# Running the gate and val products of a fused attention and SwiGLU kernel in the quarters of the TensorE array

## The chip, the core and the metric

The kernel runs on one core of one Trainium2 chip. Times are device microseconds of one launch; where a kernel was run several times, the median is given. The profile is one further execution, taken by the hardware profiler; its span reaches from the first to the last instruction and is a little shorter than the time of the launch.

## What is computed

Sigmoid attention over 8 batches, 12 heads, 448 positions and head size 64, and then a SwiGLU block over the 3584 rows that come out of it:

```python
scores = scale * np.matmul(q, k.transpose(0, 1, 3, 2)) - np.log(S)   # S = 448
attn = 1.0 / (1.0 + np.exp(-scores))
x = np.matmul(attn, v)                     # -> 3584 x 768, heads side by side
g = x @ w_gate                             # 768 x 1536
silu = g * (1.0 / (1.0 + np.exp(-g)))
out = (silu * (x @ w_val)) @ w_out         # w_out 1536 x 768
```

Inputs and output are fp32; the products run in 16-bit types and accumulate in fp32.

## The kernel before

The work is cut into small operations (a group of matmuls, one activation, one transfer). Each is noted with its engine, an assumed duration, what it depends on and which buffers it takes and gives back. A list scheduler in the kernel then orders them for each engine at build time, and they are issued in that order[...].

TensorE is used in two ways. Scores and the product of attention with v contract or emit only 64, so four matmuls of 64x64 run side by side in the quarters of the array:

```python
def burst(ds):                     # scores of one or two blocks of 64 keys, 4 heads
    for i, s in ds:
        sc = psum.tile([128, 2, 512], FP32, tag="A", bufs=2, name="ps_sc")
        for g in range(2):
            for a in range(2):
                r = slice(64 * a, 64 * a + 64)
                nc.tensor.matmul(
                    out=sc[64 * (g ^ a):64 * (g ^ a) + 64, a, 0:S]...,
                    lhsT=kT[r, s, 64 * g:64 * g + 64], rhs=qT[r, :, 64 * g:64 * g + 64],
                    start=True, stop=True)
# sig: one ScalarE sigmoid per score tile, PSUM -> pt (fp16)
# pv:  28 quarter matmuls, lhsT = v16, rhs = pt, into two banks of tag "TO";
#      then two casts make the blocks xT of x, transposed
```

The gate, val and output products use the whole array, 128 rows by 128 columns:

```python
def mm(w, nm, j0=0, j1=KC):        # KC = 6 blocks of 128 of d_model
    def fn():
        if j0 == 0:
            ...                    # T[nm, b, f] = one bank of tag "G" ("A" for the last val)
        for j in range(j0, j1):
            nc.tensor.matmul(out=T[nm, b, f], lhsT=w[c][:, j, ff * 128:(ff + 1) * 128],
                             rhs=T["xT", b, j], start=(j == 0), stop=(j == KC - 1))
    return fn
# after it: ScalarE s = sigmoid(g); VectorE t = g * s; VectorE hT = val * 1024 * t
```

The output product is a Strassen-like scheme: for every two blocks of 128 rows, seven products of six matmuls each take the place of eight. `f2_set` orders them 1, 6, 2, 7, 5, 3, 4; each lands in one bank, and one or two VectorE additions (ScalarE for the first) collect it in `osb`:

```python
def product(n, lhs, rhs, deps, final):
    ...                            # one bank of tag "TO" ("A" for odd n at the end)
    for x in range(NH):            # NH = 6
        nc.tensor.matmul(out=T["p", m, k, n], lhsT=lhs()[:, x // 2, x % 2], rhs=rhs(x),
                         start=x == 0, stop=x == NH - 1)
```

PSUM is divided as `{"A": 2 double banks, "TO": 2 banks, "G": 2 banks}`. The scheduler prefers, within limits, to stay in the mode (full array or quarters) that it is in. At the start, filling matmuls on a constant tile bridge the pauses of TensorE.

Of the kernel before, what the change touches and what calls it, by code (L numbers as in the profile page):

```python
# [19 lines left out]
class Slot:  # L20

    __slots__ = ("tag", "t1")

    def __init__(self, tag):
        self.tag, self.t1 = tag, None
# [23 lines left out]
NWARM = 6  # L49
# [7 lines left out]
VIS = 9  # L57
WO = 4
MARGIN = 1.0
FREE = set()  # L60


def list_schedule(ops, bufs, window):
# [6 lines left out]
    rings = {t: [] for t in bufs}  # L70
    turn = {t: [o for o in ops if any(s.tag == t for s in o.take)] for t in bufs if t not in FREE}
# [6 lines left out]
    def ready(o):  # L78

        r = 0.0  # L80
        for d, lead in o.deps:
            if d.t1 is None:
                return None
            r = max(r, d.t1 - lead, d.t0 + 0.01)
        ahead = {}
        for s in o.take:
            if s.tag not in FREE and turn[s.tag][0] is not o:
                return None
            ahead[s.tag] = ahead.get(s.tag, 0) + 1
            n = len(rings[s.tag]) + ahead[s.tag] - 1  # L90
            n = bufs[s.tag](n) if callable(bufs[s.tag]) else n - bufs[s.tag]
            if n >= 0:
                if n >= len(rings[s.tag]) or rings[s.tag][n].t1 is None:
                    return None
                r = max(r, rings[s.tag][n].t1)
        return r

    while left:
        later = []
        did = False  # L100
        for e, q in queues.items():
# [10 lines left out]
            for o in q[:window.get(e, 1)]:  # L112
# [8 lines left out]
                for s in o.take:  # L121
                    rings[s.tag].append(s)
# [14 lines left out]
                for s in o.give:  # L137
                    s.t1 = o.t1
# [14 lines left out]
def kernel(  # L153
# [32 lines left out]
    slots = {"A": 2, "TO": 2, "G": 2, "st": 11, "src": 2,  # L186
             "v16": 3, "qkT": 3, "pt": 10, "xT": 14, "osb": 3, "osf": 4, "S": 2}
# [36 lines left out]
    def op(*a, **kw):  # L224
        o = Op(*a, **kw)
        ops.append(o)
        return o

# [108 lines left out]
    def tr_pe(i, n, parts=None, tag="TO", split=False):  # L337
# [4 lines left out]
        def fpe(s0, s1):  # L342
            def fn():
                if s0 == 0 or split:
                    T["tr", i, n] = psum.tile([128, NS, 128], BF16, tag=tag, bufs=2, name="ps_tr")
# [13 lines left out]
        for k, (eng, s0, s1) in enumerate(parts):  # L359
            a = op("PE", 0.06 * (s1 - s0), fpe(s0, s1),  # L360
                   deps=[(ins[min(k, len(ins) - 1)], -MARGIN if i > QB else 0.0)],
                   take=[tag] if s0 == 0 or split else [], give=R["cq", i][0].take if n and s1 == NS else [])
            if s0 == 0 or split:
# [17 lines left out]
    def burst(ds):  # L381


        def fpe():
            for i, s in ds:
                sc = psum.tile([128, 2, 512], FP32, tag="A", bufs=2, name="ps_sc")
# [11 lines left out]
        if ds[0][0] == 0:  # L398
            deps = [x for k, x in R.items() if k[:2] == ("qkT", 0) and len(k) > 2 and (k[2] == 0 or k[3] <= ds[0][1])]
        a = op("PE", 0.03 + 0.19 * len(ds), fpe, deps=deps,  # L400
               mode=("Q", "Q"), take=["A"] * len(ds), give=give)
        for n, d in enumerate(ds):
            sig(d, (a, 0.19 * (len(ds) - 1 - n)), a.take[n])

    def sig(key, a, slot):
# [5 lines left out]
        R[("pt",) + key] = op("ACT", 0.89, fn, deps=[a], take=["pt"], give=[slot])  # L411

    def pv(i):
# [3 lines left out]
        def slots_of(s0, s1):  # L417
            def fn():
                if s0 == 0:
                    for a in range(2):  # L420
                        T["pv", i, a] = psum.tile([128, S], FP32, tag="TO", bufs=2, name="ps_pv")
# [17 lines left out]
        cuts = [0, 2, 5, NS] if i < QB else [0, NS]  # L439
        vc = R["v16", i]  # L440
        for s0, s1 in zip(cuts, cuts[1:]):
            a = op("PE", 0.19 * (s1 - s0), slots_of(s0, s1), deps=[(p, 0.19 * (n - s0)) for n, p in enumerate(pts[s0:s1], s0)] + [vc, R.get(("pv", i))],
                   mode=("Q", "Q"), take=["TO", "TO"] if s0 == 0 else [],
# [4 lines left out]
            if i == 1 and s0 == 0:  # L448
                a.give += warmup.take
                R["cool"] = a  # L450
        for g in range(2):
            R["xT", b, 2 * r + g] = op(eng[g], 0.54, fx(g), deps=[a], take=["xT"], give=[banks[g]])


    def f1(b, f):
        c, ff = divmod(f, FC)

        def mm(w, nm, j0=0, j1=KC):
            def fn():
                if j0 == 0:  # L460
                    if nm == "v" and b == B - 1:
                        T[nm, b, f] = psum.tile([128, 2, 512], FP32, tag="A", bufs=2, name="ps_vl")[:, 0, 0:S]
                    else:
                        T[nm, b, f] = psum.tile([128, S], FP32, tag="G", bufs=2, name="ps_" + nm)
                for j in range(j0, j1):
                    nc.tensor.matmul(out=T[nm, b, f], lhsT=w[c][:, j, ff * 128:(ff + 1) * 128],  # L466
                                     rhs=T["xT", b, j], start=(j == 0), stop=(j == KC - 1))
            return fn
# [18 lines left out]
        def product(w, nm, deps):  # L487
            deps = deps + R["w16", "w" + nm, c]
            if b or f:
                a = op("PE", 1.14, mm(w, nm), deps=xs + deps,  # L490
                       take=["A" if nm == "v" and b == B - 1 else "G"])
                return a, a.take
            a = None
            for j in range(0, KC, 2):
                a = op("PE", 0.38, mm(w, nm, j, j + 2), deps=deps + [(o, 0.19 * n) for n, (o, _) in enumerate(xs[j:j + 2])] + [a],
                       take=[] if j else ["G"])
                bank = bank if j else a.take
            return a, bank
        g, bank = product(wg16, "g", [])
        s = op("ACT", 0.45, fs, deps=[g])  # L500
        t = op("DVE", 0.54, ft, deps=[s], give=bank)

        def val():
            vv, bank = product(wv16, "v", [g] if b or f else [])
            if f == NF - 1:
                vv.give += [x for o, _ in xs for x in o.take]
            m = b // 2
            old = R["f2", m - 2] if m >= 2 and b % 2 == 0 else []
            R["hT", b, f] = op("DVE", 0.54, fh, deps=[vv, t] + old, give=bank)
# [39 lines left out]
    def f2_set(m, k):  # L549
# [6 lines left out]
        P, C = {}, {}  # L556
# [33 lines left out]
        def product(n, lhs, rhs, deps, final):  # L590
            tag = "A" if final and n % 2 else "TO"

            def fn():
                if tag == "A":
                    T["p", m, k, n] = psum.tile([128, 2, 512], FP32, tag="A", bufs=2, name="ps_ol")[:, 0, 0:HW]
                else:
                    T["p", m, k, n] = psum.tile([128, HW], FP32, tag="TO", bufs=2, name="ps_o")
# [3 lines left out]
            P[n] = op("PE", 0.975, fn, deps=deps, take=[tag])  # L601

        def add(name, n, dst, other, deps, free=True):
            C[name] = op("DVE", 0.45, lambda: nc.vector.scalar_tensor_tensor(  # L604
                out=c(*dst), in0=T["p", m, k, n], scalar=HREC, in1=c(*other), op0=MULT, op1=ADD),
                deps=[P[n]] + deps, give=P[n].take if free else [])
# [16 lines left out]
        def step1(final):  # L623
            start(final)
            product(1, lambda: blk(e, 0), lambda x: wo16[:, x, lo],
                    hs(0, NH) + [R["wo16", f] for f in range(NF)], final)

            def fn():
                for t in (e, o):
                    if final:  # L630
                        T[("osb",) + t] = staging("osf")[:, 0:DM]
                    else:
                        T[("osb",) + t] = sb.tile([128, DM], FP32, tag="osb", bufs=slots["osb"],
                                                  name=f"osb_{t[0]}_{t[1]}")
                nc.scalar.activation(out=c(e, lo), in_=T["p", m, k, 1], func=COPY, scale=HREC)
            C["p1"] = op("ACT", 0.45, fn, deps=[P[1]], take=["osf" if final else "osb"] * 2, give=P[1].take)

        def step2(final):
            w = [R["ws", 4, x] for x in range(0, NH, 2)]
            product(6, lambda: T["s", 2, m, k], lambda x: wsum(2, x), [C["s2"]] + w, final)  # L640
            add("u2", 6, (e, hi), (e, lo), [C["p1"]])

        def step3(final):
            product(2, lambda: blk(e, 1), lambda x: wo16[:, NH + x, lo], hs(NH, NF), final)
            C["s4"] = op("DVE", 0.56, lambda: nc.vector.tensor_tensor(
                out=blk(e, 1), in0=blk(e, 1), in1=T["s", 2, m, k], op=SUB), deps=[P[2], C["s2"]])
            add("c11", 2, (e, lo), (e, lo), [C["u2"]])
            if end:
                store(e, [C["c11"]], [], final, lo)

        def step4(final):
            product(7, lambda: blk(o, 0), lambda x: wsum(3, x), [C["s3"]], final)
            add("u3", 7, (o, lo), (e, hi), [C["u2"]])

        def step5(final):
            product(5, lambda: T["s", 1, m, k], lambda x: wsum(1, x), [C["s1"]], final)
            add("u4", 5, (e, hi), (e, hi), [C["u3"]], free=False)
            add("c22", 5, (o, hi), (o, lo), [C["u3"]])
            P[5].give = C["s1"].take
            if end:  # L660
                store(o, [C["c22"]], [], final, hi)

        def step6(final):
            product(3, lambda: blk(e, 1), lambda x: wo16[:, NH + x, hi], [C["s4"]], final)
            add("c12", 3, (e, hi), (e, hi), [C["u4"]])
            store(e, [C["c11"], C["c12"]], C["p1"].take[:1], final, hi if end else slice(0, DM))

        def step7(final):
            product(4, lambda: blk(o, 1), lambda x: wsum(4, x), hs(NH, NF), final)
            add("c21", 4, (o, lo), (o, lo), [C["u3"], C["c22"]])  # L670
# [173 lines left out]
```

## Time and profile before

| | |
|---|---|
| time, median of 3 runs (lowest, highest) | 419.56 us (419.51, 420.84) |
| time of the profiled run, its span | 419.31 us, 417.5 us |
| granted TensorE clock | 1.0 throughout |
| first gate product starts, last matmul starts | 25.0 us, 413.0 us |
| HBM read, written | 47.19 MB, 11.01 MB |

The page lists for each engine its busy time, its share of the span and its instructions; PEld is the loading of weights into the array, which lies beside the matmuls. A later part follows the chain of work that ended last back from the last instruction, with its shares by engine and by line. Each group line gives the source line, engine, operation, output and input tiles, shapes, count, busy time and mean length of one, and then the idle time of the engine before them.

[...] The next matmul starts long before it ends. The rate of TensorE is therefore read from the distance of starts, not from lengths.

### The profile page before, as it was taken

Reading aid. Unit: us, or ns where it says so; the run is one execution under the profiler, and the core shown is the slowest. Engines: PE = TensorE matmul, PEld = TensorE weight load, DVE = VectorE, ACT = ScalarE, POOL = GpSimd, SP = SyncE. Lnnn points to the kernel's source line nnn. Section 1 sums busy time; section 2 is a strip of 40 time slices with the busy share of each in tenths; the row PEclk is TensorE's granted clock in tenths of the full one; section 3 lists DMA queues with packets and bytes.
Section 4 is the critical chain, followed back from the end, with each engine's and each line's share of the span. In section 5 each row is a group of like instructions: output and inputs, shape, how many; then the busy total and the mean of one; then the engine's idle time right before and its main releaser. Section 6 shows DMA issues by size and latency. Waiting matters only on the chain.

```text
span 417.5 us, 7938 instructions
## 1 busy us (share of the span) xinstructions
PE 409.9 (98%) x3192; PEld 205.4 (49%) x3194; DVE 237.5 (57%) x420; ACT 217.5 (52%) x290; POOL 132.7 (32%) x196
## 2 busy tenths in 40 slices
PE   8989999999999999999999999999999999999995
PEld 3444444444445555544455454554544545555663
DVE  3445544456665775564564745647556465565873
ACT  6977777878775103577445465455455552122000
POOL 1878865753454021433031431403400100000000
PEclk9999999999999999999999999999999999999999
DMA  8999999997977026387067383472500302020235
GB/s 293 379 376 376 375 311 318 330 302 213 231 199 176 2 77 155 133 189 206 9 168 141 112 250 58 141 174 69 113 2 0 77 2 75 2 75 0 63 91 152
DMA packets 64693, 66.97 MB, mean 160 GB/s; under 512 B 35536, under 2 KB 60880, under 8 KB 64656
## 3 DMA queue, kind: packets, MB, share of 16 engines
q1 hardware_dynamic: 62704, 59.39, 49.0%
q0 software_dynamic: 1632, 6.69, 6.5%
q8 instruction: 25, 0.41, 0.4%
q10 hardware_dynamic: 320, 0.39, 0.3%
q14 instruction: 12, 0.10, 0.1%
HBM read 47.19 MB, written 11.01 MB: 139 GB/s over the span
## 4 chain that ended last, share of the span: by engine, by line
PE 93%; ACT 5%; DVE 1%; issue 0%; ACTq 0%
PE ps_g L466 26%; PE ps_v L466 24%; PE ps_o L599 18%; PE ps_sc L391 9%; PE ps_pv L426 7%; PE ps_ol L599 5%; ACT pt L408 4%; PE ps_vl L466 3%; PE ps_warm L696 1%; PE ps_tr L348 1%; DVE t L476 0%; ACT s L472 0%; DVE st L604 0%; ACT qkT L231 0%; ACT xT L231 0%
## 5 line engine op out<-in xcount | busy, mean ns | idle before, releaser
L408 ACT ACTIVATE pt<-ps_sc,sbiast 128x896 f16<-128x896 f32 x168 | 158.7, 1007 | 26.2 <-PE ps_sc L391 26.0
L466 PE MATMUL ps_g<-xT,wg 128*128 128x448 f16 x576 | 124.2, 353 | 0.8 <-DVE t L476 0.8
L472 ACT ACTIVATE s<-ps_g 128x448 f16<-128x448 f32 x96 | 52.2, 543 | 123.6 <-PE ps_g L466 122.7
L476 DVE TENSOR_TENSOR t<-ps_g,s 128x448 f16<-128x448 f32 x96 | 59.9, 624 | 92.1 <-ACT s L472 92.0
L466 PE MATMUL ps_v<-xT,wv 128*128 128x448 f16 x504 | 109.6, 354 | 0.0
L466 PEld LDWEIGHTS <-wg 128*128 128x128 f16 x576 | 54.9, 98 | 55.3 <-issue 7.4
L466 PEld LDWEIGHTS <-wv 128*128 128x128 f16 x576 | 52.2, 98 | 58.6 <-issue 16.9
L482 DVE SCALAR_TENSOR_TENSOR hT<-ps_v,t 128x448 f16<-128x448 f32 x84 | 52.4, 624 | 30.7 <-PE ps_v L466 29.9
L235 POOL CAST src<-st 128x896 bf16<-128x896 f32 (+1 forms) x43 | 40.1, 933 | 93.7 <-DMA st<-in_q_dram 60.1
L391 PE MATMUL ps_sc<-qkT 64*64 64x448 bf16 x672 | 50.9, 361 | 1.1 <-ACT pt L408 0.7
L599 PEld LDWEIGHTS <-hT 128*128 128x128 f16 x384 | 37.5, 98 | 27.2 <-issue 0.4
L235 POOL CAST v<-st 64x448 f16<-64x448 f32 (+1 forms) x72 | 42.4, 588 | 23.0 <-DMA st<-in_v_dram 8.6
L614 POOL DMA_DIRECT2D out_dram<-osb x34 | 17.7, 525 | 95.5 <-DVE osb L604 95.4
L604 DVE SCALAR_TENSOR_TENSOR osb<-ps_o,osb 128x384 f32<-128x384 f32 x63 | 33.8, 551 | 9.1 <-PE ps_o L599 9.1
L426 PE MATMUL ps_pv<-pt,v 64*64 64x448 f16 x672 | 37.0, 350 | 0.0
L233 DVE CAST xT<-ps_pv 128x448 f16<-128x448 f32 x40 | 23.5, 620 | 19.6 <-PE ps_pv L426 19.6
L599 PE MATMUL ps_o<-wo,hT 128*128 128x384 f16 x168 | 31.9, 327 | 0.0
L391 PEld LDWEIGHTS <-qkT 64*64 64x64 bf16 x672 | 15.0, 105 | 30.2 <-issue 25.7
L599 PE MATMUL ps_o<-st,hT 128*128 128x384 f16 x138 | 26.2, 327 | 0.0
L599 PE MATMUL ps_o<-st,s 128*128 128x384 f16 x138 | 26.2, 327 | 0.0
L426 PEld LDWEIGHTS <-v 64*64 64x64 f16 x672 | 19.3, 107 | 13.2 <-issue 2.6
L599 PEld LDWEIGHTS <-s 128*128 128x128 f16 x168 | 16.4, 98 | 11.8
(44 smaller groups left out, 194.4 us busy)
## 6 DMA issues: line engine op xcount, KB each, us to landing
st<-in_q_dram SPq DMA_DIRECT2D x24, 448.0 KB, 5.1
st<-in_v_dram SPq DMA_DIRECT2D x24, 448.0 KB, 6.3
st<-in_k_dram SPq DMA_DIRECT2D x23, 448.0 KB, 5.6
out_dram<-osb POOLq DMA_DIRECT2D x34, 192.0 KB, 3.1
st<-in_moe_w_gate_dram SPq DMA_DIRECT2D x12, 384.0 KB, 9.1
st<-in_moe_w_val_dram SPq DMA_DIRECT2D x12, 384.0 KB, 9.0
st<-in_moe_w_out_dram SPq DMA_DIRECT2D x12, 384.0 KB, 7.0
out_dram<-st SPq DMA_DIRECT2D x16, 192.0 KB, 2.8
```

Of the source, the lines that this page charges most:

```text
L233: nc.vector.tensor_copy(out=o, in_=i)
L235: nc.gpsimd.tensor_copy(out=o, in_=i)
L391: nc.tensor.matmul(out=sc[64 * (g ^ a):64 * (g ^ a) + 64, a, 0:S].rearrange("k (s p) -> k s p", s=NS), lhsT=kT[r, s, 64 * g:64 * g + 64], ...
L408: nc.scalar.activation(out=pt, in_=T[("sc",) + key][:, :, 0:S], func=SIGM, bias=sb_t, scale=qkscale)
L426: nc.tensor.matmul(out=T["pv", i, a][64 * g:64 * g + 64, :], lhsT=T["v16", i][r, a, s, :], rhs=T["pt", i, s][r, a, :], start=(s == 0), sto ...
L466: nc.tensor.matmul(out=T[nm, b, f], lhsT=w[c][:, j, ff * 128:(ff + 1) * 128], rhs=T["xT", b, j], start=(j == 0), stop=(j == KC - 1))
L472: nc.scalar.activation(out=t, in_=T["g", b, f], func=SIGM)
L476: nc.vector.tensor_tensor(out=t, in0=T["g", b, f], in1=T["s16", b, f], op=MULT)
L482: nc.vector.scalar_tensor_tensor(out=T["hT", m][:, f, o * S:(o + 1) * S], in0=T["v", b, f], scalar=HSC, in1=T["t1", b, f], op0=MULT, op1=MULT)
L599: nc.tensor.matmul(out=T["p", m, k, n], lhsT=lhs()[:, x // 2, x % 2], rhs=rhs(x), start=x == 0, stop=x == NH - 1)
L604: C[name] = op("DVE", 0.45, lambda: nc.vector.scalar_tensor_tensor(out=c(*dst), in0=T["p", m, k, n], scalar=HREC, in1=c(*other), op0=MULT, ...
L614: dma.dma_start(out=out[rows, cols].rearrange("(p s) d -> s p d", s=NS)[s], in_=T[("osb",) + t][64 * x:64 * x + 64, cols])
```

## The change

The change has four parts.

1. The gate and val products of a batch and a block of 128 hidden units become one pair that runs in the array's quarters (all batches but the last). A full 128x128 matmul is cut into four of 64x64. In the first half of the pair, the upper rows of the array work for gate and the lower ones for val; in the second half they swap. So the two row halves never write the same bank at the same time. Between the halves, a nop on ScalarE waits for the last matmuls of the first half, and the second half waits for the nop. Other work can be issued between the halves.
2. Output products are paired in the same way, two at a time, except in the last quarter of the rows and for single ones left over.
3. All eight PSUM banks become four double banks of one kind, and each operation that needs PSUM takes whichever the planned order frees first. The filling matmuls at the start write into the unused 64 columns of a score tile.
4. The issue order is new: scores one block at a time, spread between the other products (each not before the sigmoid of the one before it is nearly done in the plan), pv cut after four of seven blocks, the first output product copied twice by ScalarE, wider windows for ScalarE and VectorE in the scheduler.

It is meant to let TensorE stay in the quarter mode, instead of changing between full array and quarters with each group of scores or pv.

The diff, cut to its core:

```diff
-    slots = {"A": 2, "TO": 2, "G": 2, "st": 11, "src": 2,
+    slots = {"A": 2, "P": 4, "st": 11, "src": 2,
...
+    def double(name):
+        return psum.tile([128, 2, 512], FP32, tag=f"P{R['now'].got('P')[0].n}", bufs=1, name=name)
...
+    def turn(a, n):
+        def fn():
+            e = {"DVE": nc.vector, "ACT": nc.scalar, "POOL": nc.gpsimd}[TURN]   # TURN = "ACT"
+            T["turn", n()] = e.nop().ins
+            for x in T["half", n()]:
+                after_ins(T["turn", n()], x)
+        return op(TURN, 0.07, fn, deps=[a])
+
+    def quarters(steps, t, n):
+        for k, two in enumerate(steps):
+            for row in range(2):
+                o, w, x = two[row ^ t]
+                rs = slice(64 * row, 64 * row + 64)
+                for col in range(2):
+                    cs = slice(64 * col, 64 * col + 64)
+                    mm = nc.tensor.matmul(out=o[cs], lhsT=w[rs, cs], rhs=x[rs], start=t == 0 and k == 0,
+                                          stop=t == 1 and k == len(steps) - 1)
...                                # last step of half 0 -> turn -> first step of half 1
-            for n, ds in enumerate(bursts(i, sl)):
...
-        g, bank = product(wg16, "g", [])
+        if b < B - 1:
+            a = None
+            for t in range(2):
+                a = op("PE", 0.19 * KC, both(t), mode=("Q", "Q"), take=[] if t else ["P"],
+                       deps=xs + [a and turn(a, ...)] + old + R["w16", "wg", c] + R["w16", "wv", c])
+            g = v = a
+        else:
+            g = op("PE", 1.14, mm(wg16, "g"), deps=xs + R["w16", "wg", c], take=["P"])
...
+                pairs = [((one, 1), (one, 2)), ((one, 6), (one, 7)), ((one, 5), (one, 3)), ((one, 4), (two, 1)),
+                         ((two, 2), (two, 6)), ((two, 7), (two, 5)), ((two, 3), (two, 4))]
...
-            T["warm"] = psum.tile([128, 512], FP32, tag="G", bufs=2, name="ps_warm")
+        for _ in range(7 * n):
+            nc.tensor.matmul(out=T["last"][:, 0, S:512], lhsT=wide[:, 0:128], rhs=wide[:, 0:512 - S], start=True, stop=True)
...
-    window = {"PE": 40, "ACT": 12, "DVE": 16, "POOL": 8, "SP": 1}
+    window = {"PE": 40, "ACT": 30, "DVE": 40, "POOL": 8, "SP": 1}
```

## The prediction

> **What bounds the kernel now.** I read the page first: busy times, then the chain that ended last. The chain says which engine sets the end.
>
> ```profile
> PE 409.9 (98%) x3192; PEld 205.4 (49%) x3194; DVE 237.5 (57%) x420; ACT 217.5 (52%) x290; POOL 132.7 (32%) x196
> ...
> PE 93%; ACT 5%; DVE 1%; issue 0%; ACTq 0%
> PE ps_g L466 26%; PE ps_v L466 24%; PE ps_o L599 18%; PE ps_sc L391 9%; PE ps_pv L426 7%; PE ps_ol L599 5%; ACT pt L408 4%; PE ps_vl L466 3%; PE ps_warm L696 1%; PE ps_tr L348 1%; DVE t L476 0%; ACT s L472 0%; DVE st L604 0%; ACT qkT L231 0%; ACT xT L231 0%
> ```
>
> TensorE is the path for 93% of the span; ScalarE's 5% is the start, where the sigmoids pace everything. But "98% busy" hides what TensorE does between products, since records overlap. So next the timeline of TensorE, 67 to 75 us (start, length, what, how many):
>
> ```profile
> 67.90 1.31 PE L466 MATMUL ps_g<-xT,wg 128*128 128x448 f16 x6
> 69.14 1.52 PE L426 MATMUL ps_pv<-pt,v 64*64 64x448 f16 x28
> 70.48 0.55 PE L391 MATMUL ps_sc<-qkT 64*64 64x448 bf16 x8
> 70.97 1.31 PE L466 MATMUL ps_v<-xT,wv 128*128 128x448 f16 x6
> 72.11 1.30 PE L466 MATMUL ps_g<-xT,wg 128*128 128x448 f16 x6
> 73.34 0.57 PE L391 MATMUL ps_sc<-qkT 64*64 64x448 bf16 x8
> 73.84 1.31 PE L466 MATMUL ps_v<-xT,wv 128*128 128x448 f16 x6
> ```
>
> Read the starts. From the val product at 70.97 to the gate product at 72.11 it is 1.14 us: six full-array matmuls at 0.189 us, back to back. From the gate product at 72.11 to the scores at 73.34 it is 1.23: the same six and 0.09 more. The eight score matmuls (64*64, four side by side in the array's quarters, so two steps of 0.189 = 0.38) take 0.50 until the next product: 0.12 more. The 28 matmuls of pv take 1.34, seven steps of 0.189 and a little. So a quarter step of four matmuls costs what one full matmul costs, and **each change between full array and quarters costs about 0.1 us**. Over the whole trace, after the first gate product, I count 70 changes into quarters with 93 ns more than a plain step, and 70 out of them with 109 ns more.
>
> Then the waits, to see whether anything else holds TensorE (in total, times, longest):
>
> ```profile
> ACT s L472 <- PE ps_g L466: 122.7, 80, 4.8
> DVE t L476 <- ACT s L472: 92.0, 87, 2.2
> PE ps_g L466 <- DVE t L476: 0.8, 2, 0.5
> PE ps_sc L391 <- ACT pt L408: 0.7, 2, 0.4
> ```
>
> The others wait for TensorE; TensorE hardly waits for them.
>
> **A sum that must close first.** The first gate product starts at 25.02 us. After it come 576 gate and 576 val matmuls at 0.189 (217.7 us), 588 score and 596 pv matmuls, four at a time (27.8 + 28.2), 588 output matmuls at 0.163 (95.8; two such products start 0.97 us apart, six matmuls) and 28 transposes at 0.056 (1.6): 371.1 us. The 140 changes cost 6.5 + 7.6, the second step after each entry into quarters 24 ns more (1.7), two stalls 1.1. 25.0 + 371.1 + 14.1 + 1.7 + 1.1 = 413.0, and the last matmul starts at 413.0 in the trace. The last addition and store fill the rest to 417.5. The measured median, 419.56, lies 2.06 above that span.
>
> [...] semaphore instructions on ScalarE take 17 ns and lie inside the run of a 1.0 us sigmoid. [...]
>
> **The change, part by part.** I list the built program's TensorE instructions and price them with the durations above.
>
> *Products.* Gate and val of seven of eight batches become 84 pairs of 48 quarter matmuls: 4032/4 x 0.189 = 190.5 us. The 34 paired output products are 1632/4 x 0.163 = 66.5. What stays full: the last batch (144 x 0.189 = 27.2) and 30 output products (180 x 0.163 = 29.3). With scores 27.4, pv 27.8 and transposes 1.6, the sum after the first gate matmul is 370.3 us. The arithmetic is not faster at all.
>
> *Changes of mode.* 141 in the built program before, after the first gate product; 19 now (transposes of the early blocks, one single output product, and the mix of last batch with pairs). 19 x 0.1 + 0.2 = 2.1 us in place of 15.8. **This is the gain, 13.7 us, all on the path.**
>
> *Start.* The sigmoids pace it as before. The first pair needs six xT blocks; before, the sixth was cast from 26.15 to 26.68, and one more sigmoid now stands ahead of that cast on ScalarE (I add 0.25). Five of six steps of the half can run before, so the stream begins in effect at 26.0.
>
> *Turns.* 118 pairs wait for a semaphore round through ScalarE between halves: 0.16 us from the end of a step to the matmul's end (350 - 189 ns), 0.05 to ScalarE (37 to 53 ns in the trace), 0.02 for the nop, some 0.1 back, and 0.1 for the weights behind it: 0.45. In the list 99 of 118 have 0.95 us or more of other matmuls between halves, 13 have 0.57 to 0.76, six only one score step of 0.19. I charge 6 x 0.25 = 1.5 us.
>
> *Banks.* Everything now takes one of four double banks. A score bank comes back 0.16 + 0.05 + 1.01 (sigmoid) + 0.1 = 1.32 us after its step. The list gives 148 scores a successor; 36 have 1.32 us or less of TensorE work before it, four under 1.2: some 2.0 us. A gate/val bank needs 0.16 + 0.04 + 0.54 + 0.03 + 0.62 + 0.62 + 0.05 = 2.06; one of 96 has only 1.71, twelve 2.08 to 2.27: 0.8 with some queueing.
>
> Sum: 26.0 + 370.3 + 2.1 + (1.5 + 2.0 + 0.8) + 4.5 (tail, unchanged) = 407.2 of span, + 2.06 = **409.3 us**, 2.4% less.
>
> **Rivals.**
> *Instruction supply.* TensorE's list grows from 6,390 to 15,112 entries. A quarter step is eight instructions (four weight loads, four matmuls): one per 23.6 ns in gate/val, one per 20.4 in output pairs, for hundreds of us. [...] Against it: runs of 40 quarter matmuls in the trace keep 189 ns to the last step. But those are 80 instructions[...]; the densest 10 us of the trace hold 264. So it stays open; I give it 13%.
> *Banks become the bound.* Four banks were sized by a planned order; if sigmoids queue on ScalarE (78.2 of 105 us busy from 30 to 135), a late bank stalls TensorE, and the 96 pairs lose 0.15 us each: 14 us, about 419. Against it: from 165 us on ScalarE and VectorE are little over half busy.
> *Turns stuck behind sigmoids.* [...] If half of the 118 lose 0.2 us: 12 us, 420. Against it: most have over 0.95 us of cover[...].
> *The gain was hidden anyway.* No: TensorE is the path, and the sum above closes only with the changes in it.
>
> **Range and chances.** Without any stall the sum is 405.0, so below 404.5 is unlikely. Doubled stalls give 413.6; one rival in part gives 419. The 2% line is 411.2, only 1.9 above my sum: faster by over 2% 0.57, within 0.30, slower 0.13.
>
> **What will show it.** (1) Quarter steps of gv 189 ns apart, of output pairs 163[...]. (2) Some 44 changes of mode in all. (3) The wait of TensorE's weight loads for ScalarE (turns) and of its score and gv products for ScalarE and VectorE (banks), together 3 to 6 us. (4) First gv matmul near 26 us, last output matmul near 402.7. (5) VectorE's and ScalarE's busy times about as before. The prediction is wrong if step time, or the sum of those waits, is off.

## The result and the profile after

The changed kernel takes **433.05 us** (median of 4 runs, 432.78 to 433.53) against 419.66 for the kernel before (4 runs): 1.031 times the time, 95% interval 1.029 to 1.034. It was predicted faster and it is slower by 3.1%. The profiled run has a span of 431.2 us. Below, *before* and *after* name the two kernels.

First the two parts of the page that the prediction started from, busy times and the chain that ended last, of the kernel after:

```profile
PE 410.1 (95%) x7555; PEld 280.4 (65%) x7555; DVE 238.2 (55%) x420; ACT 229.1 (53%) x304; POOL 131.4 (30%) x194
...
PE 86%; DVE 5%; ACT 5%; issue 2%; DMA 1%; DVEq 0%; ACTq 0%
PE ps_gv L504 41%; PE ps_o L504 16%; PE ps_pv L454 7%; PE ps_sc L416 7%; PE ps_o L659 7%; PE ps_gv L520 6%; ACT pt L435 4%; PE ps_sc L804 2%; DVE t L542 2%; DVE st L586 1%; ACT s L538 1%; DVE hT L548 1%; PE ps_tr L373 1%; DMA st<-in_q_dram 1%; DVE xT L257 1%
```

TensorE's busy time is the same as before (410.1 against 409.9) and its share of the chain fell from 93% to 86%. So TensorE is still the path, but it now waits. `ps_sc L804` in the chain is new: these are the filling matmuls of the start, which were `ps_warm L696` before. Where the waiting lies does not show here, because the chain is an average over the whole span. The sum of the prediction, made again from starts in the trace, says it (microseconds):

| part | before | predicted | after |
|---|---|---|---|
| first gate matmul starts | 25.0 | 26.0 | 40.7 |
| the stream itself, steps only | 371.1 | 370.3 | 370.2 |
| changes of mode and the slower step behind them | 15.8 | 2.1 | 3.2 |
| stalls of TensorE in the stream | 1.1 | 4.3 | 12.4 |
| tail after the last matmul's start | 4.5 | 4.5 | 4.7 |
| span | 417.5 | 407.2 | 431.2 |

The new form brings what it was meant to bring: 12.6 us less of changes and 0.9 us less of stream. The start takes 15.7 us more, the stalls 11.3 us more, the tail 0.2 more: 13.7 us in all.

**The steps are right.** TensorE's timeline of after, a stretch within a pair (start, length, what, how many):

```profile
104.82 0.35 PE L504 MATMUL ps_gv<-xT,wg 64*64 64x448 f16 x2
104.83 0.35 PE L504 MATMUL ps_gv<-xT,wv 64*64 64x448 f16 x2
105.01 0.35 PE L504 MATMUL ps_gv<-xT,wg 64*64 64x448 f16 x2
```

From 104.82 to 105.01 it is 0.19 us for four matmuls and their four weight loads; each record is 0.35 us long, so those of successive steps overlap. Over the whole trace the steps are 189 ns apart, those of output pairs 163.

**The start is wrong.** ScalarE's timeline of before shows what paced the start: 21 sigmoids in one run without a pause, 0.92 us each.

```profile
6.24 19.26 ACT L408 ACTIVATE pt<-ps_sc,sbiast 128x896 f16<-128x896 f32 x21 [0.48 <-PE ps_sc L391]
```

The same view of after. The bracket is the idle time ahead of the sigmoid and who ended it:

```profile
7.48 1.91 ACT L435 ACTIVATE pt<-ps_sc,sbiast 128x896 f16<-128x896 f32 x2 [0.68 <-PE ps_sc L416]
12.09 1.01 ACT L435 ACTIVATE pt<-ps_sc,sbiast 128x896 f16<-128x896 f32 x1 [2.70 <-PE ps_sc L416]
14.62 1.01 ACT L435 ACTIVATE pt<-ps_sc,sbiast 128x896 f16<-128x896 f32 x1 [1.53 <-PE ps_sc L416]
```

After the second sigmoid they come singly or in pairs, at first one in about 2.5 us, and ScalarE waits for scores; only from 31.15 on do 11 follow without a pause. TensorE's timeline of after shows what the scores wait for:

```profile
11.44 0.59 PE L416 MATMUL ps_sc<-qkT 64*64 64x448 bf16 x4
13.14 0.91 PE L804 MATMUL ps_sc<-wide 128*128 128x64 bf16 x14 [1.11 <-ACT pt L435]
13.98 0.59 PE L416 MATMUL ps_sc<-qkT 64*64 64x448 bf16 x4
...
17.03 0.93 PE L373 MATMUL ps_tr<-idn,src 128*128 128x128 bf16 x7
...
40.66 0.35 PE L504 MATMUL ps_gv<-xT,wg 64*64 64x448 f16 x1
```

The scores at 11.44 are read by the sigmoid that starts at 12.09 and ends at 13.10. The filling matmuls are ordered behind these scores and write into the same tile, at 13.14, after 1.11 us of idle time that this sigmoid ended. The next scores stand behind the filling in TensorE's order. So scores and sigmoids, which overlapped before, take turns. The filling needs only the 64 columns that no sigmoid reads, yet it waits for the whole tile: it starts 0.05 us after the end of the sigmoid. The trace shows the wait, not what would come without it.

The list of waits of the whole program has the same (in total, times, longest), with the turns of the pairs in its last line:

```profile
PE ps_sc L804 <- ACT pt L435: 7.4, 6, 1.6
...
PEld L504 <- ACTq L489: 1.7, 5, 0.4
```

### The profile page after: what moved, and what is told of

Same layout as the page of the kernel before. It is cut to its first block, busy times and chain, and to the rows that moved or that the text cites. A ratio compares the mean times of both kernels' runs of the same rounds, so it can differ in the third digit from the quotient of the medians.

```text
span 431.2 us, 16715 instructions
## 1 busy us (share of the span) xinstructions
PE 410.1 (95%) x7555; PEld 280.4 (65%) x7555; DVE 238.2 (55%) x420; ACT 229.1 (53%) x304; POOL 131.4 (30%) x194
## 4 chain that ended last, share of the span: by engine, by line
PE 86%; DVE 5%; ACT 5%; issue 2%; DMA 1%; DVEq 0%; ACTq 0%
PE ps_gv L504 41%; PE ps_o L504 16%; PE ps_pv L454 7%; PE ps_sc L416 7%; PE ps_o L659 7%; PE ps_gv L520 6%; ACT pt L435 4%; PE ps_sc L804 2%; DVE t L542 2%; DVE st L586 1%; ACT s L538 1%; DVE hT L548 1%; PE ps_tr L373 1%; DMA st<-in_q_dram 1%; DVE xT L257 1%
## 5 line engine op out<-in xcount | busy, mean ns | idle before, releaser
L504 PE MATMUL ps_gv<-xT,wv 64*64 64x448 f16 x2016 | 217.0, 350 | 1.0 <-issue 1.0
L504 PE MATMUL ps_gv<-xT,wg 64*64 64x448 f16 x2016 | 217.0, 349 | 0.7 <-ACT xT L255 0.2
L504 PEld LDWEIGHTS <-wg 64*64 64x64 f16 x2016 | 121.3, 107 | 29.6 <-issue 4.0
L504 PEld LDWEIGHTS <-wv 64*64 64x64 f16 x2016 | 120.3, 107 | 26.2 <-issue 1.3
L542 DVE TENSOR_TENSOR t<-ps_gv,s 128x448 f16<-128x448 f32 x96 | 59.8, 623 | 114.9 <-ACT s L538 114.6
L538 ACT ACTIVATE s<-ps_gv 128x448 f16<-128x448 f32 x96 | 52.2, 544 | 97.3 <-PE ps_gv L504 68.2
L548 DVE SCALAR_TENSOR_TENSOR hT<-ps_gv,t 128x448 f16<-128x448 f32 x96 | 59.7, 622 | 8.1 <-PE ps_gv L520 6.0
L504 PEld LDWEIGHTS <-hT 64*64 64x64 f16 x1080 | 48.3, 107 | 12.0 <-issue 2.7
L504 PE MATMUL ps_o<-wo,hT 64*64 64x384 f16 x648 | 47.8, 323 | 0.0
L504 PE MATMUL ps_o<-st,s 64*64 64x384 f16 x480 | 45.4, 323 | 0.1
L668 DVE SCALAR_TENSOR_TENSOR osb<-ps_o,osb 128x384 f32<-128x384 f32 x63 | 33.2, 551 | 12.6 <-PE ps_o L504 8.4
```

The lines of the kernel that those rows point to most:

```text
L504: mm = nc.tensor.matmul(out=o[cs], lhsT=w[rs, cs], rhs=x[rs], start=t == 0 and k == 0, stop=t == 1 and k == len(steps) - 1)
L538: nc.scalar.activation(out=t, in_=T["g", b, f], func=SIGM)
L542: nc.vector.tensor_tensor(out=t, in0=T["g", b, f], in1=T["s16", b, f], op=MULT)
L548: nc.vector.scalar_tensor_tensor(out=T["hT", m][:, f, o * S:(o + 1) * S], in0=T["v", b, f], scalar=HSC, in1=T["t1", b, f], op0=MULT, op1=MULT)
L668: nc.vector.scalar_tensor_tensor(out=c(*dst), in0=T["p", m, k, n], scalar=HREC, in1=c(*other), op0=MULT, op1=ADD)
```

## The stalls of the stream

Each of the 60 stalls in the stream of after (12.4 us) was followed to the semaphore or buffer that ended it: banks of score tiles 23 stalls, 5.2 us; banks of gate and val 11, 1.8; val products of the last batch 5, 1.8; turns between halves 5, 0.6; gaps for which no semaphore accounts 3, 1.9; the rest, in small parts, 1.1. A stall counts for a score bank here when the sigmoid that reads the bank ended some 50 ns before TensorE went on. The 26 stalls with 6.2 and 5.8 us that two expectations below name are a wider count.

The largest kind looks like this. ScalarE's timeline of after:

```profile
94.33 0.54 ACT L538 ACTIVATE s<-ps_gv 128x448 f16<-128x448 f32 x1
94.78 1.00 ACT L435 ACTIVATE pt<-ps_sc,sbiast 128x896 f16<-128x896 f32 x1
```

and TensorE's, the scores that fill the bank and, below the dots, its next user:

```profile
94.11 0.36 PE L416 MATMUL ps_sc<-qkT 64*64 64x448 bf16 x4
...
95.44 0.36 PE L416 MATMUL ps_sc<-qkT 64*64 64x448 bf16 x4
95.83 0.38 PE L504 MATMUL ps_gv<-xT,wg 64*64 64x448 f16 x2
```

The step that fills the bank at 94.11 is over at 94.30. Its sigmoid could start at 94.51 (the records end at 94.47, and the prediction read 37 to 53 ns from there to ScalarE), but a gate sigmoid has just started at 94.33, so it starts at 94.78 and ends at 95.78. The next user of the bank was due at 95.63, one step after 95.44, and starts at 95.83: a stall of 0.20 us. The bank came back 1.53 us after its step, not 1.32 as the prediction took it with ScalarE free.

## The experiments

Theories carry letters in the expectations. **A**: the start is lost because the filling matmuls wait for the sigmoid of the tile that they write into. Its rivals are B, that the new issue order (scores one block at a time) and the single kind of bank start the stream late, and C, that the low clock of TensorE at the start does. **Q**: the score banks come back late because a score's sigmoid queues behind a gate sigmoid. Its rivals are L, that the round to the sigmoid and back is itself longer, and, without a letter, that all four banks are simply in use, whatever ScalarE's order. A ratio is to the kernel before, timed on the same chip.

### Filling into a free bank

```diff
-        for _ in range(7 * n):
-            nc.tensor.matmul(out=T["last"][:, 0, S:512], lhsT=wide[:, 0:128], rhs=wide[:, 0:512 - S], start=True, stop=True)
+        free = [b for b in range(slots["P"]) if b not in held or held[b].t1 is not None and held[b].t1 <= at]
...
+        t = psum.tile([128, 2, 512], FP32, tag=f"P{b}", bufs=1, name="ps_fill")
+        for _ in range(n):
+            nc.tensor.matmul(out=t[:, 0], lhsT=wide[:, 0:128], rhs=wide, start=True, stop=True)
```

> The same plan as the changed kernel; only the filling matmuls at the start write, 512 columns wide, into a double bank that is free at that moment in the plan, not into the spare columns of the last score tile. Theory A (the fill waits until the sigmoid has read the score tile, and the next score waits behind the fill): the first gate/val matmul goes from 40.7 back to 26 to 28 us, ScalarE's sigmoids stand back to back from about 6 us on, and the time falls by 12 to 15 us to about 419.5 (417.5 to 421.5). Theory B (the slow start comes from the new order of scores and from one kind of bank): the first gate/val matmul stays later than 36 us and the time above 428.

Measured: 420.9 us (20 runs, 419.09 to 424.63; ratio 1.0032, 1.0016 to 1.0047). TensorE's timeline has the first gate matmul at 28.34 instead of 40.66:

```profile
28.34 0.35 PE L504 MATMUL ps_gv<-xT,wg 64*64 64x448 f16 x1
```

That is a little later than expected: the sigmoids still pause three times, 1.5 us in all. The stalls are almost those of after, 59 with 11.2 us. In the profiled runs the span is 13.4 us shorter than that of after, and 12.3 of it is the start. The cause is the bank that the filling writes into: planned order and kind of bank are the same in both, which speaks against B. The filling matmuls are also wider and fewer here (512 columns in place of seven times 64).

### No filling

```diff
-            if warm_now and "last" in T and o.t0 - end > FILL:
-                fill(int((o.t0 - end - FILL) / 0.215) + 1)
```

> The same plan; no filling matmuls after the first six. Theory A (waiting fills are the loss): with no fill nothing waits for a sigmoid but what uses its result; TensorE may run at half clock at the start (transposes 107 ns apart), yet the sigmoids of 0.89 us set the pace, so the first gate/val matmul comes at 27 to 31 us and the time is 419 to 424. Theory C (the low clock of TensorE at the start is the loss, and fills are needed against it): the first gate/val matmul comes at 38 us or later and the time is 430 or more.

Measured: 418.99 us (0.998, 0.9973 to 0.9988), first gate matmul at 26.99. ScalarE's and TensorE's timelines of this kernel:

```profile
7.59 19.86 ACT L435 ACTIVATE pt<-ps_sc,sbiast 128x896 f16<-128x896 f32 x22 [0.69 <-PE ps_sc L416]
```

```profile
11.35 0.55 PE L373 MATMUL ps_tr<-idn,src 128*128 128x128 bf16 x7 [0.20 <-ACT pt L435]
```

The sigmoids are one run again, 22 of them, and the rest of the late start against before is small: they begin 1.35 us later, and there is one more. The filling is not needed for its own purpose either, which speaks against C. Seven transposes take 0.55 us here at 11.35, and 0.93 us in after at 17.03; from start to start it is about 56 ns here and 107 in after. In after they are 107 ns apart up to 19.8 us and 56 from 27.8 on. Its clock records begin only at 20.0 us and show 0.50 from 23.4 to 26.8. In before, the transposes are 107 ns apart up to 4.98 us and 56 from 5.08 on, so the clock of 1.0 in the table of before says nothing of its first 5 us. The filling of after, meant to keep TensorE at full rate, did not do that.

### Val of the last batch in its own bank

On top of filling into a free bank:

```diff
-                if nm == "g":
-                    T["gv", b, f] = double("ps_gv")
-                T[nm, b, f] = T["gv", b, f][:, "gv".index(nm), 0:S]
+                T[nm, b, f] = double("ps_" + nm)[:, 0, 0:S]
```

> As e1, but in the last batch, which runs in the full array, the val product takes a double bank of its own. In the changed kernel's trace the first val matmul there waited five times 0.32 us and once 0.48 for VectorE's product t, which reads gate in the same double bank. If that wait is the tile's, it goes and the time falls by 1.5 to 2 us against e1. If VectorE's additions for the output products limit this stage anyway, the waits move to other lines and the time falls by less than 0.5 us.

Measured: 418.38 us (0.9973, 0.9959 to 0.9987), stalls 9.5 us: 1.7 less than with the filling in a free bank alone. The median is 2.5 us less, more than expected; the profiled spans differ by 1.6. In after, five of the twelve val products of the last batch wait for VectorE's read of the gate, four times 0.32 us and once 0.48, though val lies in the other bank of the pair (TensorE's timeline; the bracket at the val product names the read):

```profile
375.75 1.68 PE L520 MATMUL ps_gv<-xT,wg 128*128 128x448 f16 x8
377.59 2.43 PE L520 MATMUL ps_gv<-xT,wv 128*128 128x448 f16 x12 [0.16 <-DVE t L542]
```

The line is L520, the full-array form of the last batch. With a bank of its own for val, the wait is gone.

### Full array for everything

This is the other side of the change: filling in a free bank, four double banks and the new order, but all gate, val and output products in the full array.

```diff
-        if b < B - 1:
+        if False:
...
-            if m == B // 2 - 1 or not sets:
-                pairs = [((one, 1), (one, 2)), ((one, 6), (one, 7)), ((one, 5), (one, 3))] if m < B // 2 - 1 else []
+            if True:
+                pairs = [((one, 1), (one, 2)), ((one, 6), (one, 7)), ((one, 5), (one, 3))] if False else []
```

> As e1, but gate, val and all output products run in the full array; the four double banks and the rule for the order of scores stay. 316 changes of mode stand in the built program in place of 44. If a change costs 0.1 us as read from the kernel before, and quarters save what I took them to save, this run is 20 to 30 us slower than e1 (about 440 to 450). If the quarters bring next to nothing, and the losses of the changed kernel come from its turns between halves, it is within 8 us of e1 or faster.

Measured: 474.29 us (one run), more than expected. The expectation left out that, with gate and val apart, all val products can meet the wait just told. It does not isolate the changes of mode, as the list of waits shows:

```profile
PE ps_gv L520 <- ACT s L538: 20.3, 58, 0.9
PE ps_gv L520 <- DVE t L542: 6.7, 26, 0.5
```

The next variant therefore has every val in a bank of its own, and no filling.

> As e6, but gate, val and all output products run in the full array, and here each val product has a double bank of its own, so that it doesn't wait for the gate's sigmoid as in e3. 306 changes of mode stand in the built program in place of 44. With 0.1 us a change the changes alone cost 26 us more than e6; a plain change is read as the start of a step 0.09 to 0.11 us late. I expect 435 to 447 us. If it comes within 8 us of e6, the quarters save nothing here.

Measured: 436.88 us (one run). TensorE's timeline:

```profile
202.28 0.38 PE L416 MATMUL ps_sc<-qkT 64*64 64x448 bf16 x4
202.60 1.31 PE L518 MATMUL ps_g<-xT,wg 128*128 128x448 f16 x6
203.84 0.38 PE L416 MATMUL ps_sc<-qkT 64*64 64x448 bf16 x4
204.15 1.31 PE L518 MATMUL ps_v<-xT,wv 128*128 128x448 f16 x6
```

From the scores at 202.28 to the product at 202.60 it is 0.32, where a step is 0.19; from there to the scores at 203.84 it is 1.24, where six steps are 1.13. Over the stream there are 290 changes, 30.9 us above plain steps (106 ns each), and 0.2 us of other stalls. With the new order of scores, the quarters (the next kernel) thus save some 20 us. The order before held its changes at 140, so against it the saving is smaller.

### Both repairs together

```diff
-            if warm_now and "last" in T and o.t0 - end > FILL:
-                fill(int((o.t0 - end - FILL) / 0.215) + 1)
...
+                T[nm, b, f] = double("ps_" + nm)[:, 0, 0:S]
```

> No fills after the first six and the val product of the last batch in a bank of its own: e2 and e4 together. Both gains stand at different ends of the run (first gate/val matmul at 27.0 against 28.3 us; about 1.6 us of stalls in the last batch), so they should add: 417.0 to 418.0 us, 0.4 to 0.7% under the kernel before. If the fills' absence costs clock later or the last stage is held by VectorE, it is no better than 418.4.

Measured: **417.12 us** (5 runs, 416.84 to 418.41; ratio 0.9947, 0.9934 to 0.9961), faster than both kernels: 0.5% below before, and 3.7% below after (417.12/433.05). The page's first line:

```profile
PE 401.4 (97%) x7422; PEld 274.4 (66%) x7422; DVE 236.0 (57%) x420; ACT 228.0 (55%) x304; POOL 133.0 (32%) x194
```

The first gate matmul is at 26.3, near the 26.0 that was predicted for the change itself. Against before: start 1.3 more, stream 0.9 less, changes 12.5 less, stalls 9.4 more (10.5 in all, of them 24 on score banks with 5.4 and three with 1.5 that no semaphore explains), tail 0.2 more: 2.5 us less of span. This is where the rest of the expected gain went. The variants that follow are made from this kernel.

### A short gate sigmoid

The gate sigmoid works on 64 of 448 columns; for the others VectorE multiplies with a constant 0.5. The output is not the reference's.

```diff
-            nc.scalar.activation(out=t, in_=T["g", b, f], func=SIGM)
+            t = T["s16", b, f] = half[T["ns"] % 2]
+            nc.scalar.activation(out=t[:, 0:64], in_=T["g", b, f][:, 0:64], func=SIGM)
```

> As e6, and the gate sigmoid on ScalarE works on 64 of its 448 columns; the rest of its tile holds 0.5 (so the output is not the reference's). The plan and the order are the same. In e1 26 stalls, 6.2 us, waited for the bank of a score tile. Theory Q (the score's sigmoid stands behind a gate sigmoid on ScalarE, so the bank comes back 0.2 us later than a free ScalarE would give it): those stalls fall below 2 us in sum and the time by 4 to 6 us against e6. Theory L (the round from TensorE to the sigmoid and back is itself longer than I took it): those stalls stay above 4.5 us, and the time falls by less than 2.

Measured: 411.5 us (0.9809, 0.979 to 0.9829), 5.6 us less than without this. ScalarE's groups of costly instructions, of the kernel with val in its own bank and of this one (busy us and mean ns after the bar, then idle time):

```profile
L536 ACT ACTIVATE s<-ps_gv 128x448 f16<-128x448 f32 x84 | 45.7, 544 | 68.9 <-PE ps_gv L504 66.8 <-PE ps_sc L416 1.1
```

```profile
L540 ACT ACTIVATE half<-ps_gv 128x64 f16<-128x64 f32 x84 | 18.8, 224 | 71.1 <-PE ps_gv L507 67.8 <-DVE hT L650 0.9
```

A gate sigmoid now takes 224 ns, and the stalls on score banks fall from 24 to 3, from 5.4 to 0.5 us. All stalls together fall from 10.5 to 6.1. Q holds for this kind, and L does not: nothing else about scores and their sigmoids was changed. (The gate and val banks also come back 0.32 us earlier, so the whole 5.6 us cannot be put down to the queue.)

### The score's sigmoid first

Can the gain be had without leaving work out? In the planned order, a gate sigmoid (`f1.` in the code) now stands back when a score's sigmoid (`sig.`) becomes ready within 0.25 us.

```diff
+                if e == "ACT" and "f1." in o.fn.__qualname__:
+                    soon_pt = [x for x in (ready(y) for y in q[:window["ACT"]] if "sig." in y.fn.__qualname__)
+                               if x is not None and now + 1e-9 < x <= now + 0.25]
+                    if soon_pt:
+                        later.append(min(soon_pt))
+                        continue
```

> As e6, but in the plan ScalarE leaves a gate sigmoid waiting when a score's sigmoid will be ready within 0.25 us, so that score banks come back sooner. If score banks are the only tight ones, the 26 stalls behind them (5.8 us in e6) go, and the time falls to 412 to 414 us. If all four banks are tight, the gate/val banks now come back about 0.9 us later each time and the stalls move there: the time rises to 419 to 424 us.

Measured: 420.95 us (1.0027, 1.0017 to 1.0038), slower by 3.8 us than without it. The stalls are 13.7 us; they moved to pv, which waits for sigmoids (8 stalls, 4.2 us), to scores that wait for a bank of scores (3.3), and to the banks of gate and val. So Q is right about what delays a score bank, yet with this rule the wait only moves. The rival had put the moved waits at the banks of gate and val; the largest single part came at pv instead. The rule changes the whole plan, so the run shows that this rule gains nothing, not that no order would.

### Three double banks

```diff
-    slots = {"A": 2, "P": 4, "st": 11, "src": 2,
+    slots = {"A": 2, "P": 3, "st": 11, "src": 2,
```

> As e6 with three double banks in place of four; the plan is made anew for it. If the remaining stalls come from too few banks, waits for banks grow from about 9 us to 30 or more and the time to 440 to 455 us. If banks are not what the stalls come from (turns, instruction supply), the time stays under 425.

Measured: 454.31 us (one run), 37 us more than with four. There are 127 stalls, 43.9 us. Two lines of the waits:

```profile
PE ps_sc L416 <- ACT pt L435: 10.1, 29, 1.4
```

```profile
PEld L504 <- ACTq L489: 9.2, 24, 0.5
```

The first are scores that wait for a bank. The second are turns between halves: with fewer banks there is less other work to put between two halves, and the turns show too. So a bank fewer costs much. That a bank more would take the remaining stalls away is argued, not shown: no run has five double banks.

## Why the prediction was wrong

*Start*, the step that failed. "The sigmoids pace it as before", and so "the stream begins in effect at 26.0". It began at 40.7: 14.7 us of the 24.0 us by which the span was missed; the stalls make another 8.1. The prediction named step time and waits as what would prove it wrong, and not this larger part. The description of the change lists that the filling matmuls moved into a score tile, but the prediction priced them at nothing. In the kernel before they had a bank of their own; here they waited for the sigmoid of the tile, and the next scores waited behind them, so that the sigmoids no longer set the pace. The first two experiments show it: with another bank for them the start is 28.3, without them 27.0. What is then left is near what the prediction said: 26.0 against 27.0 and, in the best variant, 26.3.

*Banks*, mis-sized. Score banks were put at 2.0 us and cost 5.2, gate and val banks at 0.8 and cost 1.8. The plan's distances were read rightly, but the chain was taken with ScalarE free; a wait of 0.2 us for a gate sigmoid was enough, since the plan places many next users just where 1.32 us would do. The rival "Banks become the bound" described this: it charged 14 us for them, and 7.0 came in after. So it holds in kind and for half in size.

*Missing from the sum.* The last batch's val products wait for VectorE's read of the gate in the same double bank: 1.8 us. Gaps that no semaphore explains: 1.9 us. In the sum itself two terms are slightly off: the profiled run before lies 1.81 us above its span (419.31 against 417.5), not 2.06, and the parts of a turn add up to 0.43, not 0.45.

*Turns* were put at 1.5 us and cost 0.6. The way back to TensorE was the author's estimate, 0.1 us; in after, where TensorE waits for a turn, the next weight load starts 0.05 us after the nop. The rival of turns stuck behind sigmoids is refuted: 43 of the 118 nops (17 ns each) lie inside the run of an instruction of ScalarE, up to 0.98 us after its start, and only five turns stalled TensorE. No run has such pairs without turns, so whether they need them is not shown.

*Changes of mode* were right: the gain was to be 13.7 us on the path and is 12.6. *Stream* was right to 0.1 us. The rival of *instruction supply* is refuted as a rate: 189 and 163 ns hold for hundreds of microseconds at eight instructions a step, one in 20.4 ns at the densest. *The gain was hidden anyway* is refuted too: the full-array variant is about 20 us slower than the best one.

Of the signs listed, (1), (2) and (5) came out as said, though ScalarE's busy time rose by 5%. Sign (3), 3 to 6 us of waits, did not: turns and banks have 7.6. Nor did (4): the first gate matmul came at 40.7 and the last matmul at 426.5, in place of 26 and 402.7.

## What to carry to other kernels

A matmul that does no useful work still has a place in TensorE's order and a bank that it writes, so ask of each which reader it waits for and what stands behind it (here 1.11 us of waiting, with the next scores behind it); give it a bank that nobody reads (first gate matmul at 28.3 us instead of 40.7). When a pool of buffers is sized from a plan, take the chain that returns a buffer with its queue on the shared engine, not with that engine free (1.53 us against 1.32 at 94 us), and count how many next users come within a few tenths of a microsecond of its end. A change that trades one cost that is counted easily (changes of mode) for tighter buffers should be judged by both, since here, even with the start repaired, 9.4 of the 12.5 us won went back as stalls.

## What was not expected

TensorE stands still at times where no semaphore is waited for. After, in the middle of a half pair:

```profile
269.72 0.38 PE L504 MATMUL ps_gv<-xT,wv 64*64 64x448 f16 x2 [0.98 <-issue]
```

and without filling, in the middle of one group of four scores:

```profile
59.56 0.35 PE L416 MATMUL ps_sc<-qkT 64*64 64x448 bf16 x1
60.86 0.38 PE L416 MATMUL ps_sc<-qkT 64*64 64x448 bf16 x3 [0.95 <-issue]
```

The four matmuls of this group share one bank pair and one set of inputs, so no buffer explains it. There are 0.1 to some 2 us of such gaps in a trace of the quarter form, and none in that of the kernel before or of the two full-array variants. Nor are they scattered: in four variants TensorE stops near 60 us (two matmul starts 0.8 to 1.6 us apart, where at most 0.19 is usual), and in five near 256 us (0.4 to 0.9 us). They may come from the supply of instructions, whose number has more than doubled on TensorE, but no run tests that, and their cause stays open.
